# The residual of a channel MLP reaches token layout by block transposes on VectorE and small transfers, not by transposes on TensorE

## The chip, the cores and the metric

The kernel runs on one core of one Trainium2 chip. The metric is the device time of one execution in microseconds (us); of several runs the median is given. A profile is taken of one further execution; its span goes from the first to the last instruction of the program. TensorE is called PE, VectorE DVE, ScalarE ACT, GpSimd POOL and SyncE SP, as the profile does. SP does no arithmetic here; it issues transfers, in order.

## The reference

An attention block with a threshold, followed by a mixer block, all in float32 (the mixer's weights come as float64):

```python
# q, k, v: (8, 8, 576, 64)
scores = scale * q @ k^T
thresh = max(scores) - tau
scores = where(scores >= thresh, scores, -1e9)
attn   = softmax(scores)
x      = (attn @ v) as (8, 576, 512)        # batch, token, channel
# mixer; w_tok1 (576, 256), w_tok2 (256, 576), w_ch1 (512, 1536), w_ch2 (1536, 512)
h   = relu(x^T @ w_tok1) @ w_tok2
u   = x + h^T                               # the residual of the next line
out = u + relu(u @ w_ch1) @ w_ch2
```

## The kernel before

**Units.** The main loop (L568) runs over 144 units: 18 for each of the eight batches, a unit being 128 query rows of a pair of heads. For a unit `scores` lets PE multiply q and k (L303) into two PSUM buffers `sc`, DVE takes the row maximum `mx` (L308), POOL makes the bias (L309). `weigh` has ACT apply threshold and exponential (L318, L325), `norm` has DVE and POOL normalize (L332 to L336). Two units later `turn_blocks` turns the weights `e` into `T` on DVE (L366), 32x32 blocks at a time. After every third unit, sixteen transfers on SP's queue (L375) move the blocks to their partitions in `eT`, which has one buffer. Two units on, `values` multiplies eT with v on PE (`pv`, L409 and L414). The first batch is turned on PE instead (L354).

**The mixer beside it.** Once a batch's attention is done, `push` puts its mixer steps into a queue `todo`, each with a cost near its time in us. `fill(share)` takes steps from it, at several places in a unit, up to a quota per unit, so that PE has work while DVE, POOL and ACT treat the scores. The steps are the token MLP (`turn_x`, `tok1`, `tok2`; L445, L452, L459, with an add on DVE, L463) and, for each group of 256 tokens of a pair of batches (the fifth group has 128), the channel MLP: twelve steps `ch1` (L483, 1.7 us, evicted by ACT at L484) and four steps `ch2` (L499, 2.6 us) for each 128 tokens. A group is named (batch, number) here; two groups of a pair are pushed after its even batch and three after its odd one. There are 20 groups and 36 tiles of 128 tokens. All these steps share two PSUM buffers `mm`. What is left at the end runs after the last unit, on PE nearly alone.

**The residual.** u lies in the layout of channels by tokens in `xT` (named `uT` in the channel MLP). The output is wanted by tokens. So the first `ch2` step of a tile lets PE transpose u's four 128x128 parts into the PSUM buffer (L495), the products of `ch2` are accumulated on top (L499), DVE copies the sum to a tile `o` (L504), of which there are two, and SP sends it out (L505).

**The weights.** They come in 31 pieces through four raw buffers in `scratch` (`load_piece`, SP, L177) and are converted in 93 small steps: ACT at L192 and L194 (which writes the helper `h2`), DVE at L202, L204 (the last to read `h2`) and L208, POOL at L216, which frees the raw buffer. `weight` emits these steps, two at a time in three places of a unit in the second batch, so the last pieces arrive within that batch. `h2` uses the two buffers of tag "o".

Every engine and queue carries out its instructions in the order in which the program emits them; the order is written out by hand in this loop.

Of the kernel before, what the change touches and what calls it, by code (L numbers as in the profile page):

```python
# [9 lines left out]
F32 = mybir.dt.float32  # L10
# [7 lines left out]
P = 128  # L18
# [3 lines left out]
def kernel(  # L22
# [25 lines left out]
    nc = tc.nc  # L48
    B, H, S, D = q.shape
    DM = H * D  # L50
# [10 lines left out]
    NCC = DM // P  # L61
    NJ = DCH // P
    HS = S // 2
    NK = 2 * S // P
    GR = 2 * P
# [4 lines left out]
    work = ctx.enter_context(tc.tile_pool(name="work", bufs=2))  # L70
# [39 lines left out]
    def load_v(n):  # L110

        b, p = pairs[n]
        lv = ld.tile([P, NK, D], F32, tag="lv", bufs=4, name=f"lv_{n}")
        nc.sync.dma_start(out=lv, in_=v[b].rearrange("h s d -> (h s) d")[2 * S * p : 2 * S * p + 2 * S, :].rearrange("(c p) d -> p c d", p=P))
        vals[n] = lv

    vals = {}
    ident = const.tile([P, P], F32, name="ident")
# [8 lines left out]
    wc2 = const.tile([P, NJ, DM], F32, name="wc2")  # L127
# [8 lines left out]
    WMAX = 512  # L136
    scratch = work.tile([P, NP * 2 * S], U32, tag="xT", name="scratch")
    NRAW = 4
    raw_at = [scratch[:, 2 * WMAX * i : 2 * WMAX * (i + 1)] for i in range(NRAW)]

    def like(x, dst):
        if len(dst.shape) == 2:
            return x
        return x.rearrange("p (a b) -> p a b", a=dst.shape[1])
# [23 lines left out]
    def load_piece(i):  # L168
        if i >= len(pieces):
            return  # L170
        dst, src = pieces[i]
        rows = dst.shape[0]
        n = 1
        for d in dst.shape[1:]:
            n *= d
        raw = raw_at[i % NRAW][0:rows, 0 : n * (2 if wide(i) else 1)].bitcast(src.dtype)
        nc.sync.dma_start(out=like(raw, dst), in_=src)  # L177
        if wide(i):
            words = raw.bitcast(U32).rearrange("p (n w) -> p n w", w=2)
            h2 = work.tile([P, WMAX], F32, tag="o", name=f"h2_{i}")[0:rows, 0:n]  # L180
            raws[i] = like(words[:, :, 0], dst), like(words[:, :, 1], dst), like(h2, dst)
        else:
            raws[i] = like(raw, dst)

    def wide(i):
        return i < len(pieces) and pieces[i][1].dtype == I64
# [37 lines left out]
    def weight(n):  # L224

        nonlocal steps_done
        for k in range(steps_done, min(steps_done + n, 3 * len(pieces) + 1)):
            i, part = divmod(k, 3)
            if part == 0:
                on_gpsimd(i - 1)  # L230
                if i:
                    load_piece(i - 1 + NRAW)
            else:
                on_scalar(i + 1, part - 1)
            on_vector(i, part)
            steps_done = k + 1
# [5 lines left out]
    def need(i):  # L242

        weight(3 * i + 4 - steps_done)

    load_piece(0)
    load_v(0)
    for i in range(1, NRAW):
        load_piece(i)
# [27 lines left out]
    def in_blocks(b):  # L277
        return b > 0
# [60 lines left out]
    GU = 3  # L339
# [86 lines left out]
    def token_mlp(b, ps=range(NP)):  # L426
# [42 lines left out]
        steps += [(0.97, lambda c=c, f=f: tok2(c, f)) for c in ps for f in range(2)]  # L469
        return steps, (first, first + NTK)  # L470

    def channel_mlp(b, uT, i):

        s = {}
        n = min(GR, 2 * S - GR * i)

        def ch1(j):
            need(7 + j)
            if j == 0:
                s["g"] = work.tile([P, NJ, GR], F32, tag="g", bufs=1, name=f"g_{b}_{i}")  # L480
            ps = ps_mm.tile([P, GR], F32, tag="mm", name=f"c1_{b}_{i}_{j}")[:, 0:n]
            for c in range(NCC):
                nc.tensor.matmul(ps, lhsT=wc1[:, j, c, :], rhs=uT[:, c, GR * i : GR * i + n], start=(c == 0), stop=(c == NCC - 1))  # L483
            nc.scalar.activation(out=s["g"][:, j, 0:n], in_=ps, func=AF.Relu)  # L484

        def ch2(t, part):
            need(7 + NJ + 3 * part + 2)
            t0 = GR * i + P * t
            if part == 0:
                s["ps"] = ps_mm.tile([P, NCC, P], F32, tag="mm", name=f"c2_{b}_{i}_{t}")  # L490
            ps = s["ps"]
            flat = ps.rearrange("q c d -> q (c d)")
            if part == 0:
                for c in range(NCC):
                    nc.tensor.matmul(  # L495
                        ps[:, c, :], lhsT=uT[:, c, t0 : t0 + P], rhs=ident, is_transpose=True, start=(c == 0), stop=False, skip_group_check=True
                    )
            for j in range(3 * part, 3 * part + 3):
                nc.tensor.matmul(  # L499
                    flat, lhsT=s["g"][:, j, P * t : P * t + P], rhs=wc2[:, j, :], start=False, stop=(j == NJ - 1), skip_group_check=True  # L500
                )
            if part == 3:
                o = work.tile([P, DM], F32, tag="o", name=f"o_{b}_{i}_{t}")
                nc.vector.tensor_copy(out=o, in_=flat)  # L504
                nc.sync.dma_start(out=out[b : b + 2].rearrange("b s d -> (b s) d")[t0 : t0 + P, :], in_=o)  # L505

        return [(0.0067 * n, lambda j=j: ch1(j)) for j in range(NJ)] + [
            (2.6 if part else 3.0, lambda t=t, part=part: ch2(t, part)) for t in range(n // P) for part in range(4)
        ]

# [43 lines left out]
    def values_due(u):  # L556
        while due and due[0][0] <= u:
            _, b, p0, g = due.popleft()
            values(b, p0, g)
            if b == 0 and p0 == 0 and g == 2:  # L560
                return True
            if p0 == NP - 2 and g == 2:
                if not in_blocks(b):
                    return True
                push(b)
        return False

    for u in range(len(units) + LAG + 4):  # L568
        on = u < len(units)
        if u == UB:  # L570
            late.close()
            ps_mm = ctx.enter_context(tc.tile_pool(name="ps_mm", bufs=2, space=bass.MemoryType.PSUM))
        if on:
            b_now, p0, t = units[u]
            n = b_now * NP + p0
        w = u - LAG
        back = 0 <= w < len(units)
        if on:
            scores(u)

        last = False
        visit = False
        if due and not in_blocks(due[0][1]):
            visit = due[0][0] <= u
            last = values_due(u)
        elif early:
            early.popleft()[1]()
        if 0 < u <= len(units):
            norm(u - 1)
        if b_now:  # L590
            weight(2)
        else:


            weight_to(2.25 * (u - (1 if visit else 1.5)))
            if visit and on:
                weigh(u)
        while copies:
            copies.popleft()()
        if last and u < UB:  # L600
            early.extend(token_mlp(0, range(NP // 2))[0])
        elif last:
            push(0)
        if back:
            wb, wp, wt = units[w]
            if not in_blocks(wb):
                for i in range(3):
                    turn(w, i)
            if wt % GU == GU - 1:
                g = wt // GU  # L610
                if g < 2:
                    split_middle(wb * NP + wp + g)
                due.append((u + (2 if in_blocks(wb) else 1), wb, wp, g))
        if b_now:
            fill(0.4)
        if back and in_blocks(wb):
            turn_blocks(w)
        if b_now:
            weight(2)
        if on and (b_now or not visit):  # L620
            weigh(u)
        elif b_now:
            fill(0.6)
        if b_now:
            weight(2)
        elif u == 0:
            on_scalar(0, 0)
            on_scalar(0, 1)
        else:
            weight_to(2.25 * (u - 1))  # L630
        if on:


            when = {3: (2, 0, 2), 4: (2, 2, 4), 5: (2, 4, 6), 6: (2, 6, 8), 8: (3, 0, 3), 0: (1, 3, 6), 1: (1, 6, 8)}
            if u == 0:
                load_qk(1, (nc.sync, nc.sync), range(0, 3))
            if t in when:
                m, lo, hi = when[t]
                if n + m < len(pairs):
                    load_qk(n + m, (nc.scalar if b_now else nc.sync,) * 2, range(lo, hi))  # L640
            if t in (3, 7) and n + 2 + t // 4 < len(pairs):
                load_v(n + 2 + t // 4)
            if t == 2:
                prep(n + 1)
            if t == 7 and n + 2 < len(pairs):
                prep(n + 2)
        if due and in_blocks(due[0][1]):
            values_due(u)
    need(len(pieces) - 1)
    quota = 1e9  # L650
    fill(1.0)
# [28 lines left out]
```

## Time and profile before

| | |
|---|---|
| median of 3 runs | 1363.84 us (1360.34 to 1365.55) |
| the profiled execution: own time, span | 1359.68 us, 1357.6 us |
| mean granted PE clock | 0.992 |
| PE busy | 1314.2 us (97%) |
| DVE, ACT, POOL busy | 576.6 us (42%), 585.5 us (43%), 354.1 us (26%) |
| PE transposes of u, L495 | 144, of 272 to 329 ns |
| DVE copy of the output, L504 | 36, 687 ns each |
| DVE block transposes T, L366 | 126, 1365 ns each |
| transfers eT<-T on SP, L375 | 672, median 602 ns to issue, 2.3 us to landing |
| other transfers on SP | weights 31, v 32, output 36, q and k 39 |

Busy time is the union of an engine's instructions; matmuls overlap, so the time that one adds to a row of them is read from start to start. SP has no busy time in the page: how long its queue is occupied is read from its timeline. The first 170 us hold the first batch, and 170 to 290 us the second, in which the conversion of the weights ends. The last unit starts at about 1153 us, and after 1190 us PE works on the rest of the queue.

### The profile page before, as it was taken

Reading aid. Unit: us, or ns where it says so; the run is one execution under the profiler, and the core shown is the slowest. Engines: PE = TensorE matmul, PEld = TensorE weight load, DVE = VectorE, ACT = ScalarE, POOL = GpSimd, SP = SyncE. Lnnn points to the kernel's source line nnn. Section 1 sums busy time; section 2 is a strip of 40 time slices with the busy share of each in tenths; the row PEclk is TensorE's granted clock in tenths of the full one; section 3 lists DMA queues with packets and bytes.
Section 4 is the critical chain, followed back from the end, with each engine's and each line's share of the span. In section 5 each row is a group of like instructions: output and inputs, shape, how many; then the busy total and the mean of one; then the engine's idle time right before and its main releaser. Section 6 shows DMA issues by size and latency. Waiting matters only on the chain.

```text
span 1357.6 us, 17717 instructions
## 1 busy us (share of the span) xinstructions
PE 1314.2 (97%) x6246; PEld 816.6 (60%) x6246; DVE 576.6 (42%) x1008; ACT 585.5 (43%) x1300; POOL 354.1 (26%) x683
## 2 busy tenths in 40 slices
PE   6888999999999999999999999999999999999998
PEld 4555656547474656655665566565756576576675
DVE  6889864454444434443333454434333443201000
ACT  6776655445454444543434445343434444120010
POOL 4565643222322222221212222221212222100000
PEclk8998999999999999999999999999999999999999
DMA  5435774545453533533254445435333442400000
GB/s 122 117 95 134 198 166 98 128 95 118 104 127 79 131 90 89 131 80 86 66 119 93 103 98 117 96 75 117 89 92 73 116 98 70 111 0 16 8 16 16
DMA packets 278872, 128.21 MB, mean 94 GB/s; under 512 B 200896, under 2 KB 271552, under 8 KB 278784
## 3 DMA queue, kind: packets, MB, share of 16 engines
q1 hardware_dynamic: 150176, 111.06, 32.1%
q10 hardware_dynamic: 128608, 16.01, 7.4%
q8 instruction: 50, 0.82, 0.3%
q14 instruction: 38, 0.31, 0.1%
HBM read 43.25 MB, written 9.44 MB: 39 GB/s over the span
## 4 chain that ended last, share of the span: by engine, by line
PE 86%; DVE 6%; DMA 2%; ACT 2%; SPq 2%; issue 1%; POOL 1%; ACTq 0%; DVEq 0%; POOLq 0%
PE c L499 27%; PE c L483 26%; PE sc L303 10%; PE pv L414 8%; PE t L452 5%; PE t L459 4%; PE pv L409 3%; SPq L375 2%; DVE mx L308 2%; PE tx L445 1%; PE c L495 1%; DMA lk<-in_k_dram 1%; ACT e L318 1%; ACT e L325 1%; PE tr L354 1%
## 5 line engine op out<-in xcount | busy, mean ns | idle before, releaser
L308 DVE TENSOR_REDUCE mx<-sc 128x1 f32<-128x576 f32 x288 | 204.3, 750 | 482.8 <-PE sc L303 482.8
L483 PE MATMUL c<-xT,wc 128*128 128x256 f32 (+1 forms) x1920 | 400.1, 362 | 0.5 <-ACT g L484 0.4
L499 PE MATMUL c<-wc,g 128*128 128x512 f32 x864 | 390.6, 597 | 0.0
L483 PEld LDWEIGHTS c<-xT,wc 128*128 128x128 f32 x1920 | 334.1, 190 | 71.0 <-issue 30.8
L309 POOL TENSOR_SCALAR bias<-mx,toff 128x1 f32<-128x1 f32 x288 | 82.0, 285 | 779.4 <-DVE mx L308 724.7
L318 ACT ACTIVATE e<-sc,bias 128x576 f32<-128x576 f32 x288 | 199.5, 740 | 157.5 <-POOL bias L309 154.8
L499 PEld LDWEIGHTS c<-wc,g 128*128 128x128 f32 x864 | 157.4, 190 | 175.4 <-issue 173.7
L484 ACT ACTIVATE g<-c 128x256 f32<-128x256 f32 (+1 forms) x240 | 87.1, 363 | 321.6 <-PE c L483 295.2
L325 ACT ACTIVATE e<-e,ntau 128x576 f32<-128x576 f32 x288 | 221.0, 771 | 0.0
L336 POOL TENSOR_SCALAR e<-e,rr 128x576 f32<-128x576 f32 x288 | 215.1, 760 | 14.7 <-DVE rr L333 3.0
L303 PE MATMUL sc<-kT,qT 64*128 64x288 f32 (+1 forms) x1280 | 190.5, 432 | 12.4 <-DVE kT L285 7.1
L366 DVE STREAM_TRANSPOSE T<-e 128x1152 f32<-128x1152 f32 x126 | 172.0, 1365 | 6.1 <-DMA eT<-T 3.7
L303 PEld LDWEIGHTS sc<-kT,qT 64*128 64x128 f32 (+1 forms) x1280 | 105.3, 177 | 98.7 <-issue 60.6
L414 PE MATMUL pv<-eT,lv 128*64 128x384 f32 (+1 forms) x1024 | 137.2, 408 | 0.0
L414 PEld LDWEIGHTS pv<-eT,lv 128*64 128x64 f32 x1024 | 75.6, 138 | 50.4 <-issue 40.9
L504 DVE COPY o<-c 128x512 f32<-128x512 f32 x36 | 24.7, 687 | 170.0 <-PE c L499 170.0
L419 ACT COPY xT<-pv 128x384 f32<-128x384 f32 (+1 forms) x56 | 21.0, 400 | 166.4 <-PE pv L414 165.3
L459 PE MATMUL t<-w,a 128*128 128x288 f32 x256 | 75.7, 423 | 5.7 <-DVE xT L463 4.8
L452 PE MATMUL t<-x_sb,w 128*128 128x512 f32 (+1 forms) x180 | 72.4, 549 | 0.0
L463 DVE TENSOR_TENSOR xT<-xT,t 128x288 f32<-128x288 f32 x64 | 28.4, 447 | 86.7 <-PE t L459 86.2
L459 PEld LDWEIGHTS t<-w,a 128*128 128x128 f32 x256 | 46.4, 194 | 28.4 <-issue 11.7
L325 ACT ACTIVATION_READ_ACCUMULATOR e<-e,ntau 128x1 f32 x288 | 56.7, 197 | 0.0
(43 smaller groups left out, 548.5 us busy)
## 6 DMA issues: line engine op xcount, KB each, us to landing
eT<-T SPq DMA_DIRECT2D x672, 108.0 KB, 2.3
scratch<-in_moe_w_ch_dram SPq DMA_DIRECT2D x24, 512.0 KB, 3.8
lv<-in_v_dram SPq DMA_DIRECT2D x32, 288.0 KB, 3.3
out_dram<-o SPq DMA_DIRECT2D x36, 256.0 KB, 2.2
lk<-in_k_dram ACTq DMA_DIRECT2D x111, 72.0 KB, 2.7
lq<-in_q_dram ACTq DMA_DIRECT2D x106, 72.0 KB, 2.3
lq<-in_q_dram SPq DMA_DIRECT2D x22, 72.0 KB, 3.4
lk<-in_k_dram SPq DMA_DIRECT2D x17, 72.0 KB, 3.4
```

The source lines that it names most:

```text
L303: nc.tensor.matmul(sc[h][rows, f, 0:HS], lhsT=qT[r, cols], rhs=kT[r, HS * f : HS * f + HS], start=True, stop=True)
L308: nc.vector.tensor_reduce(out=mx[:, c], in_=sc[h][:, :, 0:HS], axis=AX.XY, op=ALU.max)
L318: nc.scalar.activation(out=eh, in_=sc[h][:, :, 0:HS], func=AF.Prelu, bias=bias[:, h : h + 1], scale=SCALE, alpha=STEEP)
L325: nc.scalar.activation(out=eh, in_=eh, func=AF.Exp, bias=ntau, accum_out=rs[:, h : h + 1])
L336: nc.gpsimd.tensor_scalar(out=eh, in0=eh, scalar1=rr[:, h : h + 1], scalar2=1.0, op0=ALU.mult, op1=ALU.mult)
L366: nc.vector.transpose(out=T[:, :, place, :].rearrange("p a (c x) -> p c a x", c=NK), in_=e.rearrange("p (c a x) -> p c a x", c=NK, a=4))
L414: nc.tensor.matmul(to[r], lhsT=lv[:, j, :], rhs=e[j], start=False, stop=(c == NI - 1), skip_group_check=True)
L452: nc.tensor.matmul(to, lhsT=w1[:, t, P * m : P * m + P], rhs=x_sb[:, t, cols], start=(t == 0), stop=(t == NT - 1))
L459: nc.tensor.matmul(to, lhsT=a[:, m, P * c : P * c + P], rhs=w2[:, m, HS * f : HS * f + HS], start=(m == 0), stop=(m == NTK - 1))
L483: nc.tensor.matmul(ps, lhsT=wc1[:, j, c, :], rhs=uT[:, c, GR * i : GR * i + n], start=(c == 0), stop=(c == NCC - 1))
L484: nc.scalar.activation(out=s["g"][:, j, 0:n], in_=ps, func=AF.Relu)
L499: nc.tensor.matmul(flat, lhsT=s["g"][:, j, P * t : P * t + P], rhs=wc2[:, j, :], start=False, stop=(j == NJ - 1), skip_group_check=True)
```

## The change

At the step `ch1` number 1 of a group, DVE turns the group's u in 32x32 blocks into a tile `us` (`turn_u`). Sixteen transfers on SP (`move_u`) bring the blocks to their partitions in a tile `ut`, where tokens lie on partitions. Both tiles have one buffer. The transfers are emitted at the end of a unit whose number is one past that of an eT batch, or at a tile's last `ch2` step if that comes first, or at the end of a unit after the last scores. The PE transposes go; the first product of `ch2` starts the PSUM sum. The copy at the end becomes an addition of PSUM and `ut`, written into `us`, and the output is sent from there. To make room, `h2` moves from the two buffers of tag "o" to one place in the free tail of `scratch`.

```diff
+    high = scratch[:, 2 * WMAX * NRAW : 2 * WMAX * NRAW + WMAX].bitcast(F32)
...
-            h2 = work.tile([P, WMAX], F32, tag="o", name=f"h2_{i}")[0:rows, 0:n]
+            h2 = high[0:rows, 0:n]
...
+    moves = deque()
...
+        def turn_u():
+            us = work.tile([P, GR // P, 4, NCC * 32], F32, tag="us", bufs=1, name=f"us_{b}_{i}")
+            ut = work.tile([P, GR // P, 4, NCC * 32], F32, tag="ut", bufs=1, name=f"ut_{b}_{i}")
+            nc.vector.transpose(
+                out=us[:, 0:nt].rearrange("q n a (c d) -> q c (n a) d", c=NCC),
+                in_=uT[:, :, GR * i : GR * i + n].rearrange("q c (m r) -> q c m r", r=32),
+            )
+            s["us"], s["ut"] = us, ut
+            def move(a, k):
+                nc.sync.dma_start(out=ut[32 * a : 32 * a + 32, 0:nt, k, :], in_=us[32 * k : 32 * k + 32, 0:nt, a, :])
+            moves.extend([lambda a=a, k=k: move(a, k) for a in range(4) for k in range(4)])
...
             nc.scalar.activation(out=s["g"][:, j, 0:n], in_=ps, func=AF.Relu)
+            if j == 1:
+                turn_u()
...
-            if part == 0:
-                for c in range(NCC):
-                    nc.tensor.matmul(
-                        ps[:, c, :], lhsT=uT[:, c, t0 : t0 + P], rhs=ident, is_transpose=True, start=(c == 0), stop=False, skip_group_check=True
-                    )
             for j in range(3 * part, 3 * part + 3):
-                nc.tensor.matmul(
-                    flat, lhsT=s["g"][:, j, P * t : P * t + P], rhs=wc2[:, j, :], start=False, stop=(j == NJ - 1), skip_group_check=True
-                )
+                nc.tensor.matmul(flat, lhsT=s["g"][:, j, P * t : P * t + P], rhs=wc2[:, j, :], start=(j == 0), stop=(j == NJ - 1))
             if part == 3:
-                o = work.tile([P, DM], F32, tag="o", name=f"o_{b}_{i}_{t}")
-                nc.vector.tensor_copy(out=o, in_=flat)
+                move_u()
+                o = s["us"][:, t].rearrange("q a x -> q (a x)")
+                nc.vector.tensor_add(
+                    out=o.rearrange("q (c k d) -> q c k d", c=NCC, k=4),
+                    in0=s["ps"].rearrange("q c (k d) -> q c k d", k=4),
+                    in1=s["ut"][:, t].rearrange("q k (c d) -> q c k d", c=NCC),
+                )
...
-            (2.6 if part else 3.0, lambda t=t, part=part: ch2(t, part)) for t in range(n // P) for part in range(4)
+            (2.6, lambda t=t, part=part: ch2(t, part)) for t in range(nt) for part in range(4)
...
+    def move_u():
+        while moves:
+            moves.popleft()()
...
+        if back and wt % GU == 0 or not on:
+            move_u()
```

More of the change, by code (lines that the diff above doesn't have):

```diff
@@ L475, in channel_mlp @@
         n = min(GR, 2 * S - GR * i)
+        nt = n // P
+        def turn_u():
[9 more added lines that the diff above has]
+            moves.extend([lambda a=a, k=k: move(a, k) for a in range(4) for k in range(4)])
         def ch1(j):
@@ L490, in ch2 @@
                 s["ps"] = ps_mm.tile([P, NCC, P], F32, tag="mm", name=f"c2_{b}_{i}_{t}")
-            ps = s["ps"]
-            flat = ps.rearrange("q c d -> q (c d)")
-            if part == 0:
-                for c in range(NCC):
-                    nc.tensor.matmul(
-                        ps[:, c, :], lhsT=uT[:, c, t0 : t0 + P], rhs=ident, is_transpose=True, start=(c == 0), stop=False, skip_group_check=True
-                    )
-            for j in range(3 * part, 3 * part + 3):
-                nc.tensor.matmul(
-                    flat, lhsT=s["g"][:, j, P * t : P * t + P], rhs=wc2[:, j, :], start=False, stop=(j == NJ - 1), skip_group_check=True
-                )
-            if part == 3:
-                o = work.tile([P, DM], F32, tag="o", name=f"o_{b}_{i}_{t}")
-                nc.vector.tensor_copy(out=o, in_=flat)
+            flat = s["ps"].rearrange("q c d -> q (c d)")
+            for j in range(3 * part, 3 * part + 3):
+                nc.tensor.matmul(flat, lhsT=s["g"][:, j, P * t : P * t + P], rhs=wc2[:, j, :], start=(j == 0), stop=(j == NJ - 1))
+            if part == 3:
+                move_u()
[4 more added lines that the diff above has]
+                    in1=s["ut"][:, t].rearrange("q k (c d) -> q c k d", c=NCC),
+                )
                 nc.sync.dma_start(out=out[b : b + 2].rearrange("b s d -> (b s) d")[t0 : t0 + P, :], in_=o)
         return [(0.0067 * n, lambda j=j: ch1(j)) for j in range(NJ)] + [
-            (2.6 if part else 3.0, lambda t=t, part=part: ch2(t, part)) for t in range(n // P) for part in range(4)
+            (2.6, lambda t=t, part=part: ch2(t, part)) for t in range(nt) for part in range(4)
         ]
+    def move_u():
+        while moves:
+            moves.popleft()()
     KEEP = 45.0
```

## The prediction

> **What bounds the kernel now.** The page's first two parts come first: which engine is full, and where in the span.
>
> ```profile
> PE 1314.2 (97%) x6246; PEld 816.6 (60%) x6246; DVE 576.6 (42%) x1008; ACT 585.5 (43%) x1300; POOL 354.1 (26%) x683
> PE   6888999999999999999999999999999999999998
> ```
>
> TensorE is busy from 306 us to the end. The windows view shows it by stretch (columns: window, length, then PE, PEld, DVE, ACT, POOL busy, clock, DMA share, GB/s):
>
> ```profile
> 204.00:238.00 34.00, 32.77 (x171) 22.63 (x167) 16.79 (x28) 17.54 (x40) 10.81 (x24) 1.00 0.42 100
> 272.00:306.00 34.00, 30.75 (x126) 15.70 (x125) 17.34 (x33) 17.23 (x35) 10.15 (x24) 1.00 0.41 97
> 612.00:646.00 34.00, 34.00 (x171) 19.70 (x168) 13.08 (x24) 10.92 (x24) 6.00 (x12) 1.00 0.36 86
> ```
>
> So there are two regimes: the first 306 us, in which PE has gaps and other things set the pace, and the rest, where time taken off PE is time won. What the transposes of u cost PE is read in the timeline, start to start:
>
> ```profile
> 1310.54 0.60 PE L495 MATMUL c<-ident,xT 128*128 128x128 f32 x4
> 1310.97 10.46 PE L499 MATMUL c<-wc,g 128*128 128x512 f32 x24
> ```
>
> Four take 1310.97 - 1310.54 = 0.43 us, 108 ns each, not the 273 ns which one lasts: they overlap.
>
> Next, what the new work will queue behind. Rows of the line view and of the L375 source view (durations min/median/max ns):
>
> ```profile
> L366 DVE STREAM_TRANSPOSE T<-e 128x1152 f32<-128x1152 f32 x126 | 172.0, 1365 | 6.1 <-DMA eT<-T 3.7
> L504 DVE COPY o<-c 128x512 f32<-128x512 f32 x36 | 24.7, 687 | 170.0 <-PE c L499 170.0
> L375 SPq DMA_DIRECT2D eT<-T x672: 585/602/1962, 140.1 to 1184.3; - x168
> ```
>
> An issue on SP costs 0.6 us; sixteen take 10.3 to 14.9 us in the timeline, and the queue is in order. SP's timeline in the early stage:
>
> ```profile
> 150.86 16.24 SPq L177 DMA_DIRECT2D scratch<-in_moe_w_ch_dram  x6
> 167.32 10.31 SPq L375 DMA_DIRECT2D eT<-T  x16
> 177.75 0.52 SPq L177 DMA_DIRECT2D scratch<-in_moe_w_ch_dram  x1
> ...
> 209.84 12.13 SPq L375 DMA_DIRECT2D eT<-T  x16
> 222.08 0.53 SPq L505 DMA_DIRECT2D out_dram<-o  x1
> 231.54 12.43 SPq L375 DMA_DIRECT2D eT<-T  x16
> ```
>
> and who needs these transfers at once (the bracket is the idle time before, and what ended it):
>
> ```profile
> 154.79 0.70 ACT L192 ACTIVATE scratch<-scratch 128x512 int32<-128x512 uint32 x1 [5.21 <-DMA scratch<-in_moe_w_ch_dram]
> 162.03 0.68 ACT L192 ACTIVATE scratch<-scratch 128x512 int32<-128x512 uint32 x1
> 223.84 0.87 PE L409 MATMUL pv<-eT,vl 128*64 128x384 f32 x4 [1.23 <-DMA eT<-T]
> 246.38 0.55 PE L409 MATMUL pv<-eT,vl 128*64 128x192 f32 x4 [1.54 <-DMA lq<-in_q_dram]
> ```
>
> The reader is to see that before 306 us SP's transfers arrive just in time: PE waits at 223.84 for an eT that has landed 0.2 us earlier, and at 246.38 for one that landed 0.1 us earlier (the bracket names another DMA; the last of the sixteen landed at 246.25).
>
> **What the Trainium skill says.** "TensorE: Matmul & The Clock Gate", Part 4: PE-mode transpose, has about 275 ns for a transpose in a kernel; the trace agrees on one (273 ns) but charges 108 for each in a row, and the second number is the gain. "VectorE: DVE Perf Modes", The three transpose paths: VectorE turns 32x32 blocks and not the whole tile, which is why 16 transfers must follow; L366 with its 16 transfers of L375 is that pattern already. "DMA: Bandwidth & Descriptors", Anatomy of one DMA: a semaphore is waited for on the issuing sequencer, not in the DMA engines; the trace agrees, SP stood up to 19.8 us before an L375 until VectorE's T was done, with everything behind it.
>
> **The change part by part.** A group is 256 tokens (128 the last) of a batch pair; there are 20, with 36 output tiles. A unit is one pass of the main loop (6.5 to 15 us, from one L303 start to the next).
>
> *Removed on PE:* 36 x 4 transposes x 0.108 us = 15.6 us. After 306 us nearly all 34 us windows show PE 33 to 34 us busy, so there all of it counts; four tiles fall before (1.7 us), of which I count half: **-14.8 us**. Its bounds are 13.9 and 15.6.
>
> *Added on VectorE:* L366 and L285 (576 elements in 0.75 us, 1152 in 1.365) give 0.11 + 1.09 ns an element: 1.23 us for a full group, 0.67 for a half, 16 x 1.23 + 4 x 0.67 = 22.4 us. VectorE is 42% busy and PE has 2 us or more of other work between scores and the next use of their PSUM, which hides it except where VectorE is full (unit 23, about 143 us): **+1 us**. The add in the copy's place: L463 does 288 elements in 447 ns, so 512 make 0.68 us against 0.69: nothing.
>
> *Added on SP:* 20 x 16 issues. Not in the trace with this form (32 x 2 runs of 512 B); nearest is L375's 0.602 us, with the gaps between 0.65, so 10.4 us a group. Below it the row of L505, 0.36 (5.8 us a group); above it the slowest sixteen of L375, 14.9 us. I take 10.4. Following the queue of costs through the loop, they are put at the end of a unit, one unit after an eT batch and 1.5 before the next. SP is free between two eT batches for 9.3 to 15.3 us, so after 306 us they fit: of the 14 groups there with an eT batch behind them, none pushes it further than the slack between its landing and its pv. Two before do not fit:
> - Group (0,0), end of unit 23. SP has issued the weight loads up to 152.0; the moves hold it to 163. The load issued at 155.79 goes out at 163, lands 5 us later at 168 (as it took then), and ScalarE's L192 wants it at 162.03: 6 us of ScalarE in order, with L318 and the evictions L484 behind it. PE goes on for one step or so: **+5 us** (0 to 8).
> - Group (0,1), end of unit 32. It waits for its transpose (next item), runs 225.6 to 236, and the eT of 231.54 starts at 236: it was needed without slack: **+4.5 us** (0 to 9).
>
> *A new wait on VectorE.* us has one buffer, and the output leaves from it, so a group's transpose waits until the previous group's output has landed. Behind it in VectorE's order stand mx and T, and ScalarE's L318 waits for mx. Mostly an output goes out as the add ends and lands in 2.2 us, while PE has two ch1 steps (3.4 us) to do: hidden. Four times the output queues behind an eT batch and the transpose follows within a unit: before (0,1), issued 222.08, landed 224.3, so mx of unit 33 comes at 225.6 in place of 217.3; and before (2,0), (4,0), (6,0), 4 to 5 us each. All four delay a unit in whose end PE has the 3 to 4 us of pv, which need neither: **+2 us** for the four (0 to 8).
>
> *h2 with one buffer for two.* ScalarE's L194 of piece i+1 now waits for VectorE's L204 of piece i. In 12 of 31 pieces it started before that end, by 0.02 to 2.55 us, 10.6 us in sum, with L318 next in ScalarE's order; in several L318 would have waited for mx anyway. I take **+3 us** (0 to 9), all before 183 us.
>
> *Nothing:* the moves' 9.4 MB on engines busy a third of the time; the tail after 1190 us, where PE alone works and the moves (about 14 us with landing) have 31 us to the first add, and the last output still follows one 0.7 us instruction.
>
> **Sum:** -14.8 + 1 + 5 + 4.5 + 2 + 3 = +0.7 us on the profiled execution's own 1359.68 us (span 1357.6 and 2.1 around it). That run is 4.2 us below the median of the three, 1363.84, and near the lowest, so I move the sum to the median: **1364 us**.
>
> **The rivals.** *(A) The delays are absorbed.* SP's issues cost nearer 0.36 us, or the early stage has slack that I don't see, and of the 15.5 us of delays some 2 are left: 1363.8 - 14.8 + 2 = 1351. For it: PE is idle for only 6.4 us between 170 and 306 us, so most waits there have other work beside them. Against: slacks of 0.1 and 0.2 us at the two eT landings.
>
> *(B) Slower: SP's queue becomes the bound.* If sixteen moves cost what the slowest sixteen eT did, 14.9 us (0.93 each), they overrun the free 9.3 to 15.3 us. Past the slack of the eT behind, group by group: 2.2 (0,2), 2.3 (2,0), 2.9 (4,0), 1.7 (6,0), and 4.5 more in each of the two early ones: 18 us, 1364 + 18 = 1382. For it: L375 runs that long whenever q and k load beside it. Against: the median issue is 0.602 us, and the move has fewer runs. It decides from about 0.76 us an issue.
>
> *(C) The change gives nothing to PE* because the transposes hid under weight loads: the timeline's start-to-start excludes it.
>
> **How the numbers follow.** About 0.5% (6.8 us) is what a measurement of this kernel can tell from no change. Forecast 0.43; (A) and what lies toward it 0.29; (B) and larger early losses 0.28. Cases of both signs hold most of the chance: the forecast's own range is 1357 to 1371. The wide range runs from just under (A), 1350, to 1379, short of (B).
>
> **What would show it.** Right: no L495; PE busy down by 15 to 22 us; an SP batch of about 10.4 us after every eT batch in which a group begins; ScalarE idle some 6 us before an L192 near 162 us; the pv near 246 us some 4 us later against its unit; VectorE idle before the new transpose until out_dram has landed, near 224 us. Wrong: moves issued in under 0.45 us or over 0.75, VectorE waits that PE feels after 306 us, or an early stage (to 306 us) not about 10 to 16 us longer while the rest is 14 us shorter.

## The result, and the profile after

The changed kernel takes 1370.85 us (median of 6 runs, 1367.22 to 1372.07), the kernel before, run beside it, 1363.12 us (6 runs). The ratio is 1.0053 with a 95% interval of 1.0033 to 1.0072: slower by some 7.7 us. The profiled execution took 1367.22 us with a span of 1365.4 us.

The page's first two parts, of the kernel after:

```profile
PE 1303.6 (95%) x6102; PEld 806.9 (59%) x6102; DVE 596.1 (44%) x1028; ACT 584.9 (43%) x1300; POOL 352.5 (26%) x683
PE   5887799999999999999999999999999999999998
```

PE has 144 matmul instructions fewer and is busy 10.6 us less, yet the end comes later: what PE saved it stands idle. Slices 4 and 5 (102 to 171 us) fall from 8 and 9 to 7. The windows view of the kernel after, in the same stretches and columns as before:

```profile
204.00:238.00 34.00, 31.43 (x150) 17.36 (x148) 15.66 (x26) 13.22 (x29) 8.38 (x18) 1.00 0.48 113
612.00:646.00 34.00, 34.00 (x142) 19.16 (x142) 16.51 (x30) 12.91 (x30) 7.97 (x16) 1.00 0.49 112
```

The late stretch is full as before; the early one has lost 1.3 us of PE. The largest losses lie between 150 and 420 us (the same view, the kernel before and then the kernel after):

```profile
150.00:420.00 270.00, 262.11 (x1259) 158.36 (x1259) 137.39 (x232) 134.69 (x296) 87.84 (x168) 1.00 0.52 123
150.00:420.00 270.00, 248.89 (x1166) 152.83 (x1166) 138.39 (x229) 129.32 (x286) 85.18 (x160) 0.97 0.54 125
```

PE is idle for 21.1 us there, before for 7.9, and its granted clock is lower, 0.97 in place of 1.00. The rows of the line view and of the view of the tile `ut` for the new operations:

```profile
L520 DVE TENSOR_TENSOR us<-c,ut 128x512 f32<-128x512 f32 x36 | 24.8, 688 | 161.5 <-PE c L516 138.2 <-DMA eT<-T 20.4 <-DMA lq<-in_q_dram 2.9
L487 DVE STREAM_TRANSPOSE us<-xT 128x1024 f32<-128x1024 f32 (+1 forms) x20 | 22.6, 1131 | 50.8 <-DMA out_dram<-us 47.2 <-DVE T L367 3.5
L494 SPq DMA_DIRECT2D ut<-us x320: 507/595/2040, 154.7 to 1354.6; - x160
```

These durations are close to the forecast: 688 ns for the add, 22.6 us for all block transposes, a median of 0.595 us for one issue of a move. But a row of durations doesn't show how long SP is held by sixteen. SP's timeline at the first group does (columns: start, length, engine and line, names, number of instructions):

```profile
153.13 1.51 SPq L178 DMA_DIRECT2D scratch<-in_moe_w_ch_dram  x3
154.69 14.20 SPq L494 DMA_DIRECT2D ut<-us  x16
169.05 1.44 SPq L178 DMA_DIRECT2D scratch<-in_moe_w_ch_dram  x3
170.59 12.71 SPq L376 DMA_DIRECT2D eT<-T  x16
```

and the timelines of ScalarE and PE in the same stretch show who stood behind it:

```profile
168.01 0.48 ACT L420 COPY xT<-pv 128x384 f32<-128x384 f32 x1 [4.14 <-DMA lq<-in_q_dram]
172.49 0.65 ACT L193 ACTIVATE scratch<-scratch 128x512 int32<-128x512 uint32 x1 [4.00 <-DMA scratch<-in_moe_w_ch_dram]
173.47 3.50 PE L504 MATMUL c<-xT,wc 128*128 128x256 f32 x8 [7.57 <-ACT g L505]
```

ScalarE stood still twice. First it had to issue a load of q (166.32) and one of k (167.65): in the trace each of the two waits on a completion semaphore that a move on SP was the last to raise, and goes out as that move lands (166.30 and 167.63). So the copy L420 came 4.14 us late. Then came the weights: the piece could be issued only at 169.05, and ScalarE waited 4.0 us for it. Its eviction L505 stood behind both, and PE lost 7.57 us: the longest new wait of PE in the trace.

PE loses more there than the pause. Eight products of `ch1`, of the same shape, show it (L483 in the kernel before is L504 in the kernel after; PE's timeline of the kernel before, to be set against the line at 173.47, and then the windows view of the kernel after around that line, whose third column from the end is the clock):

```profile
171.44 1.99 PE L483 MATMUL c<-xT,wc 128*128 128x256 f32 x8 [0.41 <-ACT g L484]
```

```profile
169.80:176.50 6.70, 3.04 (x7) 2.50 (x8) 2.44 (x5) 4.01 (x9) 0.77 (x1) 0.50 0.87 258
```

They take 1.99 us before and 3.50 us at 173.47, where the granted clock is 0.50. After 150 us the trace of the kernel after has three such stretches at half clock, 13.7 us in all (from 169.7, 258.5 and 374.5), near pauses of PE of 7.57, 2.03 and 3.41 us; two other pauses of 2.1 and 2.4 us have none. The kernel before has neither such a stretch nor a pause over 1.6 us there. As an estimate, half of 13.7, some 6.8 us of PE's work, is lost in this way on top of the idle time, at most.

At the third group, (0,2), the same queue is too full; SP's timeline and then PE's:

```profile
335.48 11.28 SPq L376 DMA_DIRECT2D eT<-T  x16
346.81 14.26 SPq L494 DMA_DIRECT2D ut<-us  x16
361.17 0.53 SPq L114 DMA_DIRECT2D lv<-in_v_dram  x1
361.81 10.25 SPq L376 DMA_DIRECT2D eT<-T  x16
```

```profile
374.75 1.55 PE L410 MATMUL pv<-eT,vl 128*64 128x384 f32 x4 [3.41 <-DMA out_dram<-us]
```

`T` was ready at 356.82, its sixteen transfers started 5.0 us later because SP was still with the moves, they landed at 374.66, and PE began at 374.75 after 3.41 us of idling (the bracket names another DMA that landed about then). The last of the three stretches at half clock begins as this pause ends.

Over the 20 groups sixteen moves held SP for 254.9 us, 12.7 us on average and between 10.2 and 16.3. The view of the waits of SP's queue says why it is not 10.4. Three of its rows (total us, times, longest):

```profile
SPq L376 <- DVE T L367: 186.0, 29, 10.8
SPq L494 <- DMA lq<-in_q_dram: 49.0, 14, 6.1
SPq L494 <- DVE us L487: 25.0, 8, 5.0
```

In the middle of a batch of moves SP stands still until a load of q has landed, 49.0 us in all, 2.45 us a group: 10.2 + 2.45 = 12.65. In one of them the move stopped at 418.53 us and went on at 423.50, when a load landed (423.48) that ScalarE's queue had issued only at 420.11. In the trace that move waits on the completion semaphore that this load was the last to raise. The data of the two have nothing to do with each other. The batches of eT stop in the same way, in the kernel before too (34.5 us in 18 waits for loads of q).

### The profile page after: what moved, and what is told of

Same layout as the page of the kernel before. It is cut to its first block, busy times and chain, and to the rows that moved or that the text cites. A ratio compares the mean times of both kernels' runs of the same rounds, so it can differ in the third digit from the quotient of the medians.

```text
span 1365.4 us, 17805 instructions
## 1 busy us (share of the span) xinstructions
PE 1303.6 (95%) x6102; PEld 806.9 (59%) x6102; DVE 596.1 (44%) x1028; ACT 584.9 (43%) x1300; POOL 352.5 (26%) x683
## 4 chain that ended last, share of the span: by engine, by line
PE 84%; DVE 6%; DMA 3%; ACT 2%; SPq 2%; issue 1%; POOL 1%; ACTq 0%; DVEq 0%; POOLq 0%
PE c L516 26%; PE c L504 25%; PE sc L304 11%; PE pv L415 8%; PE t L453 5%; PE t L460 4%; PE pv L410 3%; DVE mx L309 2%; SPq L376 2%; PE tx L446 1%; ACT e L319 1%; DMA lk<-in_k_dram 1%; PE tr L355 1%; DVE wc L205 1%; DMA lq<-in_q_dram 1%
## 5 line engine op out<-in xcount | busy, mean ns | idle before, releaser
L504 PE MATMUL c<-xT,wc 128*128 128x256 f32 (+1 forms) x1920 | 401.0, 362 | 7.7 <-ACT g L505 7.6
L504 PEld LDWEIGHTS c<-xT,wc 128*128 128x128 f32 x1920 | 335.1, 191 | 77.8 <-issue 30.3
L505 ACT ACTIVATE g<-c 128x256 f32<-128x256 f32 (+1 forms) x240 | 86.5, 361 | 298.4 <-PE c L504 278.0
L367 DVE STREAM_TRANSPOSE T<-e 128x1152 f32<-128x1152 f32 x126 | 171.9, 1364 | 4.1 <-DMA eT<-T 1.6
L520 DVE TENSOR_TENSOR us<-c,ut 128x512 f32<-128x512 f32 x36 | 24.8, 688 | 161.5 <-PE c L516 138.2
L420 ACT COPY xT<-pv 128x384 f32<-128x384 f32 (+1 forms) x56 | 21.0, 400 | 172.8 <-PE pv L415 164.7
L410 PE MATMUL pv<-eT,vl 128*64 128x384 f32 (+1 forms) x256 | 47.3, 439 | 10.2 <-DMA eT<-T 4.5
```

What stands on the lines that cost most here:

```text
L367: nc.vector.transpose(out=T[:, :, place, :].rearrange("p a (c x) -> p c a x", c=NK), in_=e.rearrange("p (c a x) -> p c a x", c=NK, a=4))
L410: nc.tensor.matmul(to[r], lhsT=vl[:, r], rhs=e[NI], start=True, stop=False, skip_group_check=True)
```

## The experiments

All ratios are against the kernel before, run beside the experiment. Differences between two experiments are of their medians.

### What each part costs

*The buffer h2 alone*, in the kernel before:

```diff
+    high = scratch[:, 2 * WMAX * NRAW : 2 * WMAX * NRAW + WMAX].bitcast(F32)
...
-            h2 = work.tile([P, WMAX], F32, tag="o", name=f"h2_{i}")[0:rows, 0:n]
+            h2 = high[0:rows, 0:n]
```

> The kernel before, with h2 alone moved from two buffers to the one place in the tail of scratch (ScalarE's write of piece i+1 then waits for VectorE's last read of piece i). If the one buffer is among the costs, as the prediction has it: 3 us slower (up to 9), the units of the first batch starting later by that. If it costs nothing, as the trace after suggests (the first 21 units shift by 0.3 us after a common 1.8): within 1 us of before.

Measured: 1362.56 us against 1362.57, ratio 1.0006 (0.9994 to 1.0017). One buffer for h2 costs nothing that can be measured.

*The PE transposes out, and nothing in their place*, in the kernel before; the cost of a first ch2 step goes from 3.0 to 2.6 as in the change:

```diff
-            if part == 0:
-                for c in range(NCC):
-                    nc.tensor.matmul(ps[:, c, :], lhsT=uT[...], rhs=ident, is_transpose=True, ...)
...             # the first product of ch2 now starts the PSUM sum, start=(j == 0)
-            (2.6 if part else 3.0, lambda t=t, part=part: ch2(t, part)) ...
+            (2.6, lambda t=t, part=part: ch2(t, part)) ...
```

> The kernel before with only the 144 transposes of u on TensorE taken out (the residual is left out of the output; nothing else is changed but the cost of 3.0 us to 2.6). If TensorE is the bound and a transpose costs 0.108 us: 14 to 15.6 us faster, 1348 us. If they were covered by waits or weight loads: under 7 us faster.

Measured: 1355.76 us against 1362.57, ratio 0.9948 (0.9931 to 0.9965). Only 6.8 us come of 144 x 0.108 = 15.6 us of work removed. That is the size expected if the transposes had been covered by other waits, but the run at the other cost, below, rules that reason out.

*The changed kernel without its 320 moves*; the add reads u unturned:

```diff
-            moves.extend([lambda a=a, k=k: move(a, k) for a in range(4) for k in range(4)])
...
-                    in1=s["ut"][:, t].rearrange("q k (c d) -> q c k d", c=NCC),
+                    in1=uT[:, :, t0 : t0 + P].rearrange("q c (k d) -> q c k d", k=4),
```

> The changed kernel without the 320 transfers: VectorE still turns u into us and waits there for the previous output, and the addition reads u where it lies (so the residual in the output is not turned). If SP's queue is what costs: some 19 to 22 us less than the changed kernel, that is 11 to 14 us faster than before. If VectorE's wait for the output with mx behind it is what costs: nearly as slow as the changed kernel, no more than 5 us less.

Measured: 1355.71 us against 1362.57, ratio 0.9946 (0.9932 to 0.996), the same as without any residual. So, at this cost of a step, VectorE's 20 block transposes, the wait of `us` for its output and the add in the copy's place together cost nothing that can be measured, and the moves on SP cost 1370.85 - 1355.71 = 15.1 us. The expected 19 to 22 us were too many, because the transposes of PE gave back less than forecast.

*The first group's moves behind the weights*: in the changed kernel they are held for one eT batch more, until the last weight pieces are issued.

```diff
-        if back and wt % GU == 0 or not on:
+        if (back and wt % GU == 0 and u > 24) or not on:
             move_u()
```

> The changed kernel, but the transfers of the first group are held until unit 26, behind the last weight loads (one condition on the unit's number). If the step of 8 us between units 25 and 29 comes from the weights waiting behind these sixteen transfers: 6 to 9 us less than the changed kernel, about level with before, and ScalarE's wait of 4 us at 172 us and TensorE's of 7.6 us at 173 us gone. If it comes from VectorE's added transpose there: no change.

Measured: 1362.43 us against 1362.57, ratio 0.9997 (0.9988 to 1.0007). 8.4 us of the 15.1 lie in that one place. ScalarE's timeline in this experiment, where 172.49 stood:

```profile
167.53 0.68 ACT L193 ACTIVATE scratch<-scratch 128x512 int32<-128x512 uint32 x1
172.67 0.72 ACT L193 ACTIVATE scratch<-scratch 128x512 int32<-128x512 uint32 x1
```

Both waits of ScalarE and PE's 7.57 us before L504 are gone, and so is the long stretch at half clock from 169.7; three of 3.4 us are left in this trace.

### The cost in the queue of steps

The transposes gave only 6.8 us. The one other edit in that experiment is the cost of 2.6 in place of 3.0. *The same, with the cost left at 3.0:*

```diff
-            (2.6, lambda t=t, part=part: ch2(t, part)) ...
+            (2.6 if part else 3.0, lambda t=t, part=part: ch2(t, part)) ...
```

> As the kernel before with only the transposes of u taken out (residual left out of the output), but the cost of a tile's first ch2 step stays at 3.0, so that the quota per unit and with it the place of every step is that of the kernel before. Without the transposes and at a cost of 2.6 the gain was 7 us, with units 27 to 36 in fact 4 to 5 us later than in a run of the same early stage. If the shifted places of the steps lost that: 11 to 13 us faster than before here. If the early stage gives nothing back because transfers set its pace, whatever the places: again about 7 us, at most 9.

Measured: 1348.20 us against 1362.28, ratio 0.9904 (0.9887 to 0.992). Now 14.1 us are won, somewhat more than the 11 to 13 expected. The starts of the units say the same: against the kernel with h2 alone they come earlier by 0.43 us for each tile, steadily, to 15.1 us at the end. The cost of a step is no instruction, but `fill` decides by it after how many steps a unit stops, and so where each later step stands beside the scores. With 2.6 the waits of PE differ in many small places (before `sc` for `e` 6.1 us in place of 4.5, before `pv` for a transfer 3.9 in place of 2.1, before `t` for `g` 3.2 in place of 0.8); no single one makes the 7.6 us. That the cost constant makes the difference is shown; which of the shifted places do is not.

*The changed kernel with the cost at 3.0* (the same edit):

> The changed kernel with the cost of a tile's first ch2 step left at 3.0 (one number). If the shifted places of the steps cost the changed kernel time: 3 to 5 us less than the changed kernel, 1366. If not: within 2 us of it, 1371.

Measured: 1367.09 us against 1362.28, ratio 1.0044 (1.0028 to 1.006). Here it brings 1 to 4 us and not 7.6: the intervals of this kernel and of the changed one overlap. What one edit is worth depends on the other.

### Attempts to get the moves out of the way

*The moves ahead of the unit's q and k loads in the program*, so that they would not wait for these:

```diff
+        if back and wt % GU == 0 or not on:
+            move_u()
         if on:
             ... # loads of q, k and v
-        if back and wt % GU == 0 or not on:
-            move_u()
```

> The changed kernel with the sixteen transfers of a group emitted a few lines earlier in the same unit, ahead of the unit's loads of q and k on ScalarE's queue. If the transfers stand on SP because they share completion semaphores with those loads, which ScalarE has not issued yet (14 waits, 49 us): sixteen take 10.2 to 11 us in place of 10.2 to 16.3, the step of 7 us between units 51 and 52 goes, and the time falls by 4 to 8 us to 1363 to 1367. If it is the number of issues that fills SP: no change beyond 2 us.

Measured: 1369.43 us against 1362.28, ratio 1.0054 (1.0037 to 1.007), and the waits of moves for loads of q still sum to 49.4 us. The expectation failed: to emit the moves ahead of the unit's loads does not take these waits away.

*All three at once* (moves ahead of the loads, the first group behind the weights, and `turn_u` at ch1 number 6 in place of 1, when the last output has landed):

```diff
-            if j == 1:
+            if j == 6:
                 turn_u()
```

> The changed kernel with three edits that the traces point to: transfers ahead of the q and k loads, the first group's behind the weights, and VectorE's turn at step ch1 number 6, when the previous output has long landed. If these waits are all that stands between the changed kernel and the one without transfers (1355.7): 1355 to 1359, 4 to 8 us faster than before. If the number of issues costs as well: 1360 to 1363.

Measured: 1366.5 us (13 runs, 1358.54 to 1371.33) against 1362.28, ratio 1.003 (1.0014 to 1.0046). VectorE's wait for the output is 10.7 us in place of 47.2, all of it after the last unit, and nothing is won over the kernel with the first group moved alone (1362.43): the time lies above both ranges that were expected. That wait is free, as the run without moves had said.

*The moves right behind the eT batch of the same unit*, where they fill the gap before the next batch from its beginning:

```diff
         if back and in_blocks(wb):
             turn_blocks(w)
+            if wt % GU == GU - 1:
+                move_u()
...
-        if back and wt % GU == 0 or not on:
+        if not on:
             move_u()
```

> The changed kernel with a group's sixteen transfers emitted directly behind the next eT batch in the program, one unit earlier than the end of the unit after it (the order on SP stays: eT, then the moves, but the q and k loads of a unit and more now come later in the program). If SP stood before the moves on completion semaphores that they share with such loads: 49 us of waits on SP fall below 15, sixteen moves take 10.2 to 12 us, eT waits for SP by under 1 us, and with the first group's moves now behind all but one of the weight loads the kernel falls from 1371 to 1356 to 1361. If the number of issues is what costs: 1362 to 1364, as with the first group's moves put behind the weights alone.

Measured: 1372.66 us against 1362.97, ratio 1.008 (1.0068 to 1.0092). This is slower than both ranges that were expected, and the waits of moves for loads of q are still 49.1 us. The first group's moves now stand ahead of the last weight piece (SP issued it at 191.65), and PE's timeline has a new wait there:

```profile
197.83 2.92 PE L304 MATMUL sc<-kT,qT 64*128 64x288 f32 x8 [11.09 <-ACT e L319]
```

*The same with the cost at 3.0:*

> The same, with the cost of a tile's first ch2 step left at 3.0. If SP's waits are gone, what is left of the two losses is the places of the steps, and this one gets most of the 14 us that taking the transposes out gave at that cost: 1349 to 1355. If SP's issues or VectorE's wait for the output still cost: 1358 to 1363.

Measured: 1371.43 us (1364.49 to 1376.56) against 1362.97, ratio 1.0066 (1.0045 to 1.0086), again above both ranges, with the same step of about 11 us in the unit starts near 190 us. PE's pause there is 10.1 us long, and 10.2 us at half clock follow from 189.8.

### Fewer issues

*Both amendments that had helped*: the first group behind the weights, and the cost at 3.0.

> The changed kernel with both amendments at once: the first group's transfers held until the weights are loaded, and the cost of a tile's first ch2 step back at 3.0. Theory (the two losses lie in different places, so they add): 8.4 us for the weights and 1 to 4 us for the places of the steps come off 1370.9, so 1358 to 1361, 2 to 5 us below the kernel before, and the steps of unit starts at units 25 to 26 are gone while those at 36 to 39 and at 51 to 57 remain. Rival (whatever is taken from one batch of transfers is given back at the next, because SP has no slack left): no better than with the weights alone, 1362 to 1364.

Measured: 1365.19 us (22 runs, 1361.8 to 1369.86) against 1363.07, ratio 1.0017 (1.0006 to 1.0027). The two don't add, as the rival said; its reason, that SP has no slack left, is not shown by this run. Sixteen moves in any of these places leave the kernel between no change and slower. Sixteen took 12.0 us on average.

*In the same kernel, five transfers through DRAM for the sixteen:*

```diff
+    dram = ctx.enter_context(tc.tile_pool(name="dram", bufs=1, space=bass.MemoryType.DRAM))
...
+            ud = dram.tile([GR, DM], F32, tag="ud", name=f"ud_{b}_{i}")
-            def move(a, k):
-                nc.sync.dma_start(out=ut[32 * a : 32 * a + 32, 0:nt, k, :], in_=us[32 * k : 32 * k + 32, 0:nt, a, :])
+            def move(k):
+                if k < 4:
+                    nc.sync.dma_start(
+                        out=ud[0 : nt * P, P * k : P * k + P].rearrange("(n a r) x -> r n a x", a=4, r=32),
+                        in_=us[32 * k : 32 * k + 32, 0:nt],
+                    )
+                else:
+                    nc.sync.dma_start(out=ut[:, 0:nt].rearrange(...), in_=ud[0 : nt * P].rearrange("(n p) x -> p n x", p=P))
```

> As the kernel with both amendments, but us goes to ut through a scratch tensor in DRAM: four transfers of 32 partitions each write token rows, a fifth, which waits for the four, reads them back on 128 partitions. Five issues per group in place of sixteen, twice the bytes, all on SP's queue. Theory (SP's time for the issues is the cost): SP is held for 5 times 0.65 us and some 2 us of the fifth's wait, about 5.5 us for 12.7, so of the some 11 us that stand between the kernel with both amendments and the one without the residual (1348) about half goes: 1351 to 1356. Rival (the cost is the traffic, or waiting for completions, and not the number of issues): twice the bytes and one more wait for a landing, 1359 to 1368.

Measured: 1351.51 us (1351.01 to 1353.24) against 1363.07, ratio 0.9925 (0.9906 to 0.9944). This is faster than the kernel before and than the changed one, by 11.6 us and 19.3 us. SP's timeline at group (0,2), first with sixteen moves (the kernel with both amendments), then with five transfers:

```profile
332.38 10.91 SPq L376 DMA_DIRECT2D eT<-T  x16
343.34 15.12 SPq L494 DMA_DIRECT2D ut<-us  x16
...
359.20 10.27 SPq L376 DMA_DIRECT2D eT<-T  x16
```

```profile
328.37 11.34 SPq L377 DMA_DIRECT2D eT<-T  x16
339.76 2.15 SPq L498 DMA_DIRECT2D ud<-us  x4
345.99 0.38 SPq L503 DMA_DIRECT2D ut<-ud  x1
346.47 0.41 SPq L115 DMA_DIRECT2D lv<-in_v_dram  x1
351.37 11.61 SPq L377 DMA_DIRECT2D eT<-T  x16
```

The sixteen end at 358.46 and eT starts 3.9 us after its `T` (355.31). The five are done at 346.37, though the fifth has waited 4.1 us for the four to land, and eT starts with its `T` at 351.3. SP is held 4.7 us a group (3.6 to 7.7) in place of 12.0. In the trace with sixteen, eT starts behind its `T` by 0.9 to 4.1 us after ten of the groups; in the trace with five after none.

The Trainium skill, "DMA: Bandwidth & Descriptors", Anatomy of one DMA, puts a fixed cost of some 2 us on each transfer that GpSimd issues, most of it after the issue. The moves, issued by SP, come near it with 1.9 us from issue to landing, and the fifth transfer of a full group, of 512 KB, took 3.7. That time is hidden here, and twice the bytes are too: a transfer of eT takes 2.3 us to land in both traces. What counts is how long the issuing queue is held. Of that, the number of issues is by the traces the larger share: the waits of moves for loads of q fell from 30.9 us with sixteen to 13.9 with five, but those of eT rose from 32.9 to 52.3, so that SP's waits for these loads stay near 65 us in all. No run of its own separates the two.

The unit starts of this kernel stay within 3.4 us of those without a residual at cost 3.0, from the first unit to the last, and the only stretch at half clock after 150 us is one of 3.4 us: of 14.1 us to be won, 11.6 arrive.

## Why the prediction was right and where it was wrong

The forecast, 1364 us with its own range of 1357 to 1371, holds the 1370.85, near its upper end. The change came out slower by 0.53% where the forecast said within 0.5%. The sum +0.7 stands against +7.7, and its terms compare so:

| step of the prediction | forecast | runs |
|---|---|---|
| 144 PE transposes gone | -14.8 | -14.1 (cost left at 3.0) |
| cost of a first ch2 step 3.0 to 2.6 | not costed | +7.3 to +7.6 |
| SP: group (0,0) before the weights | +5 | +8.4 |
| SP: group (0,1), and all others | +4.5, 0 | +6.7 together |
| PE at half clock beside its pauses | not costed | within the rows above, at most 6.8 (estimate) |
| VectorE's block transposes | +1 | 0 |
| VectorE's wait for the output | +2 | 0 |
| h2 with one buffer | +3 | 0 |

These terms are each taken with the edits before them in place; the runs with the cost at 3.0 show that they don't simply add: there the way from no residual (1348.20) to the changed kernel (1367.09) is 18.9 us and not 15.1.

*The gain was right, with a condition.* Transposes start to start at 0.108 us, all on the path after 306 us: the unit starts with the cost at 3.0 show 0.43 us a tile. **The step that failed is the one left out**: the change lowers the cost constant in the list of steps from 3.0 to 2.6, the prediction does not mention it, and without the moves it took half of the gain.

*SP's queue was the right place, and mis-sized.* The price of an issue was right (0.595 us against 0.602 taken), the price of sixteen was not: 12.7 us and not 10.4. The forecast had this in its hands, since eT's sixteen took 10.3 to 14.9 in the profile before, and the moves run where loads run. After 306 us eT started behind its `T` at nine of the 14 groups, by 0.7 to 5.1 us. So the claim that none of them pushes eT past its slack failed, at (0,2), where eT started 5.0 us late and PE idled 3.41 us; (0,3) was as late, by 5.05 us, and PE had other work. Group (0,0) held the weights as described, but at 172.49 and not at 162.03; with the q and k loads that the moves held as well, which the forecast did not have, it cost PE 7.57 us and a stretch at half clock. No term of the forecast prices the clock. At (0,1) eT started 4.0 us after its `T`, as forecast.

*Three small losses were not there.* The 6 us put on VectorE and h2 were each argued from an instruction that waits longer. The waits are real (9.83 us before L487 at 233.01, 8.9 us of ScalarE's L195 for VectorE's L205), and PE had other work each time. They made up for most of what SP's terms lacked. That the sum of the losses, 15.5, agrees with the 15.1 that the moves cost is luck, and so, in part, is that the measured time lies within the forecast's range.

*The rivals.* (A), losses absorbed, is out, and so is (C), since the run with the cost at 3.0 won 14.1 us. (B) named the mechanism, SP held too long, with a price of 0.93 us a move; 12.7 / 16 = 0.79, waits included, lies between the forecast's 0.65 and that, and past the 0.76 from which (B) was to decide, and past the 0.75 named as a sign of being wrong. The pattern it foretold holds for (0,2); for (2,0), (4,0) and (6,0), where eT was 1.9 to 2.5 us late, little of it reached PE, and the whole stayed far below its 1382.

*Where the trace was to show it.* PE's busy time fell by 10.6 us, not by 15 to 22; part of that gap is products that ran at half clock and so count longer. The early stage did not end at 306 us: against the kernel with h2 alone the unit starts lose ground until about 415 us, 17 us from unit 24 to unit 57, and then win back 9.5 to the end. These are single executions: the two profiled ones end 2.7 us apart, where the medians are 8.3 us apart.

## What to carry to other kernels

A queue that issues transfers in order is a resource like an engine: price a batch by how long the timeline shows it held in that stretch, waits included, and not by the median of one issue. If it is the tight one, fewer and larger transfers can help even where they move twice the bytes and take longer to land, as five did here for sixteen. And a constant that only steers a schedule is an edit to be measured by itself: here it was worth half of the gain in the kernel without moves, and 1 to 4 us in the one with them. And a pause of PE is to be priced with the clock behind it, where the trace shows a low one there.

## What the runs showed that was not expected

- Moves on SP's queue stop for loads of another queue with which they share no data: 49.0 us in 14 waits, on completion semaphores that the loads raised last. It works the other way too: ScalarE's loads stopped for moves 8 times, for 10.2 us, with ScalarE's arithmetic behind them. Two other places for the moves in the program left 49.4 and 49.1 us. Whether other semaphores would free them was not tried.
- A pause of PE can be paid twice: after 7.57 us of idling, eight products took 3.50 us in place of 1.99, at a granted clock of 0.50. That the pause brings the low clock about is read from their places in the traces; no run varies the one alone. In the six runs of the moves right behind eT at the cost of 3.0 the time broadly follows the mean granted clock, from 1364.49 us at 0.995 to 1376.56 at 0.985.
- Two amendments that win 8.4 and 1 to 4 us alone win less together (1365.19) than the first by itself (1362.43).
- Five transfers through DRAM in place of sixteen in SBUF took SP's time from 12.0 to 4.7 us a group and the kernel from 1365.19 to 1351.51 us.
